# Column sums of a soft mixture in the logits' bank, dispatch weights turned ahead of the logits

## The chip, the core and the metric

One of the cores of a Trainium2 chip runs the whole program in fp32. The metric is device time in microseconds (us), the median of several runs. PE is TensorE, DVE is VectorE, ACT is ScalarE, POOL is GpSimd, SP is SyncE, which issues the transfers.

## The reference

Three layers follow each other. The middle of each is cut here to what is computed:

```python
attn = softmax(scale * q @ mean8(k).T);  x = attn @ mean8(v)   # 8 batches, 8 heads, 576 x 72, head size 64
r = np.maximum(x @ w_in, 0.0);  x = (r * r) @ w_out            # 4608 tokens, 512 -> 2048 -> 512
logits = x @ phi                                               # 4608 x 32 slots
d = np.exp(logits - logits.max(0));  d /= d.sum(0) + 1e-09     # over tokens
slot_input = d.T @ x                                           # 32 x 512, 4 slots for each of 8 experts
slot_out[e] = np.maximum(slot_input[e] @ w1[e], 0.0) @ w2[e]
c = np.exp(logits - logits.max(1));  c /= c.sum(1) + 1e-09     # over slots
return c @ slot_out
```

The maximum over tokens is only known at the end, so the kernel keeps a running maximum and running sums, which it rescales at each pair of tiles.

## The kernel before

**Tiles and units.** The 4608 tokens are 36 tiles (`NT`) of 128. The hidden layer of 2048 is cut into four quarters (`NQ`). A unit is one tile and one quarter: twelve 128x512 products on PE (`l1_half`, L453, weights and activations in high and low parts), then relu on ACT (L466) and the square on DVE (L473) or ACT (L475), which gives `g`. Units go two tiles at a time from tile 4 on; between them stand the other steps. The product with `w_out` is never made for a token: `phi` is folded into `w_out` (`a_sb`), and the sums over tokens are taken of `g`.

**The steps of a pair** (tiles t and t+1), each named by its function:

- `reload_turned` (L508) fetches the stored `g` back in a turned layout, `g_T` (L516) turns its 32x32 blocks on DVE.
- `logits` (L541) multiplies with `a_sb`, quarter by quarter. For tiles from 10 (`ND`) on, all quarters accumulate in the bank `pl`; then ACT copies the sum to `plsb` (L558). For tiles below 10, whose logits come late, each quarter takes a bank `att` and DVE adds it up (L556).
- `log_T` (L570) adds the four partial rows up and replicates the result with one product into the tile `lp`, in the bank `misc`. From `lp` come the maximum `m` (L573) and its running negative `nm` (L575) on DVE, the exponential `dT` with its sums `drs` (L582) and the rescaling factor `scl` (L588) on ACT, and on DVE four turns of the logits into `lt_sb` (L585) and the running sum `sn` (L590). `lt_sb` and `sn` are not needed until the end of the program; `dT` is needed at once.
- `d_T` (L605) turns `dT` in four pieces into `d`.
- `dg` (L615) multiplies `d` with the eight `g` of the pair into another tile of the bank `misc`; DVE then rescales and adds this to `acc` (L625). For the early pairs (0, 2, 4, 6 and 8) `g` has been fetched back from DRAM as `g_back`.

The names in the order of instructions below follow the tiles: `l_3717` is one tile of the bank `l1`, `pl`, `misc`, `att`, `gT` are banks, `turned` and `tmp` are buffers that hold the turned `g`.

**Banks.** PSUM has eight banks: two each for `l1`, `gT` and `att`, one for `misc`, one for `pl`.

**Attention beside it.** The tiles' attention runs in the same stream: `att_sc` (L234, L241, L245), the turning of the weights on DVE (L293), twelve block copies from there into the one buffer `aT` (`att_shift`: seven on ACT, L284, five on DVE, L286), the product with v (`att_av`, L311) and the split of its result into `xh` (L318, ACT) and `xl` (L319, DVE).

**What sets the order.** `at(slot, fn, ...)` puts a step into a numbered half unit, `run_slot` emits what is due there. The framework's scheduler then orders each engine's instructions by a simulated timeline. `tc.issue_after(x)` and, on top of it, `behind(names, fn)`, `pinned` and `behind_l1` hold a step back until another instruction, on the same engine, has been put in the order; `behind_l1` takes the last L453 product emitted so far. `post_end` sets the slots of `log_T`, `d_T` and `dg` of a pair, and puts `dg` of the pairs 10 to 26 behind such a product:

```python
        if ND <= t < NT - 8:
            at(s0 + p[2], behind_l1, dg, t)
```

**The end.** Tiles 34 and 35 are handled one by one: `log_T` of 34 uses `misc`, of 35 a bank of `l1`. After the last `acc`, PE turns it (L1010), ACT and DVE copy it to `accT` (L1014 `accT0`, L1015 `accT1`), PE multiplies with `w_out` (L1023), ACT scales the result with `rn` (L1031), and `rn` is the reciprocal of the last `sn` (L1018, L1019). From there the expert layers follow (L1046, L1078), the combination with c (L1107) and the stores of the output. Between these, `slot_weights_mm` (L650, PE) and `slot_weights_out` (L655 ACT, L656 DVE) prepare c, turned, as `cT`, and `slot_softmax` (L635 to L641) its last four tiles.

Of the kernel before, what the change touches and what calls it, by code (L numbers as in the profile page):

```python
# [8 lines left out]
F32 = mybir.dt.float32  # L9
# [3 lines left out]
ALU = mybir.AluOpType  # L13
# [4 lines left out]
def kernel(  # L18
# [12 lines left out]
    nc = tc.nc  # L31
# [3 lines left out]
    NSLOT = phi.shape[1]  # L35
# [4 lines left out]
    P = 128  # L40
    NT = NTOK // P
# [9 lines left out]
    ND = 10  # L51
# [13 lines left out]
    p2 = ctx.enter_context(tc.tile_pool(name="p2", bufs=2))  # L65
# [3 lines left out]
    ps1 = ctx.enter_context(tc.tile_pool(name="ps1", bufs=1, space=bass.MemoryType.PSUM))  # L69
# [14 lines left out]
    lt_sb = const.tile([P, NT, NSLOT], F32, tag="lt", name="lt_sb")  # L84
    acc = const.tile([P, QF], F32, tag="acc", name="acc")
# [6 lines left out]
    def ps(name):  # L92
        return ps2.tile([P, 512], F32, tag=name, name=name)

    def psm():
        return ps1.tile([P, 512], F32, tag="misc", name="misc")
# [265 lines left out]
    st_t, mark, n_st = {}, {}, [0]  # L362
# [44 lines left out]
    def natural(x):  # L407
        return x.rearrange("p (a c f) -> p c a f", a=4, f=32)
# [31 lines left out]
    hp_t, g_t, gT_t, L_t, dT_t, d_t, sc_d = {}, {}, {}, {}, {}, {}, {}  # L440
# [116 lines left out]
        elif alone or j == NQ - 1:  # L557
            nc.scalar.copy(out=dst, in_=pl)  # L558

    run, order = {}, []  # L560

    def width(t):
        return 1 if t >= NT - 2 else 2

    def log_T(t):
        w = width(t)
        order.append(t)
        pl = L_t.pop(t)[:, :w * P]
        lp = (ps("l1") if t == NT - 1 else psm())[:, :w * P]
        mark["log_T"] = nc.tensor.matmul(lp, s4rep.rearrange("p a b -> p (a b)"), pl)  # L570
        m = p2.tile([P, 1], F32, tag="m", name="m")
        nm = p2.tile([P, 1], F32, tag="nm", name="nm")
        nc.vector.reduce_max(out=m, in_=lp, axis=AX.X)  # L573
        if run:
            mark["nm"] = nc.vector.scalar_tensor_tensor(  # L575
                out=nm, in0=m, scalar=-1.0, in1=run["nm"], op0=ALU.mult, op1=ALU.min
            )
        else:
            nc.vector.tensor_scalar(out=nm, in0=m, scalar1=-1.0, scalar2=None, op0=ALU.mult)
        dT = p2.tile([P, 2, P], F32, tag="dT", name="dT")[:, :w]  # L580
        rs = p2.tile([P, 1], F32, tag="drs", name="drs")
        mark["exp"] = nc.scalar.activation(out=dT.rearrange("p u t -> p (u t)"), in_=lp, func=AF.Exp, bias=nm, accum_out=rs)  # L582
        for r in range(P // NSLOT):
            b = slice(r * NSLOT, (r + 1) * NSLOT)
            nc.vector.transpose(out=lt_sb[b, t:t + w], in_=lp[b].rearrange("p (u t) -> p u t", u=w)[:, :, b])  # L585
        if run:
            scl = p2.tile([P, 1], F32, tag="scl", name="scl")
            nc.scalar.activation(out=scl, in_=run["nm"], func=AF.Exp, bias=nm, scale=-1.0)  # L588
            sn = p2.tile([P, 1], F32, tag="sn", name="sn")
            nc.vector.scalar_tensor_tensor(  # L590
                out=sn, in0=run["s"], scalar=scl, in1=rs, op0=ALU.mult, op1=ALU.add
            )
            sc_d[t] = scl
            run["s"] = sn
        else:
            run["s"] = rs
        run["nm"] = nm
        dT_t[t] = dT

    def d_T(t):  # L600
        dT = dT_t.pop(t)
        d = p2.tile([P, 2, NSLOT], F32, tag="d", name="d")[:, :width(t)]
        for r in range(P // NSLOT):
            b = slice(r * NSLOT, (r + 1) * NSLOT)
            mark["d"] = nc.vector.transpose(out=d[b], in_=dT[b, :, b])  # L605
        d_t[t] = d

    def dg(t):
        d = d_t.pop(t)
        assert order.pop(0) == t  # L610
        dp = ps("gT") if t == NT - 1 else psm()
        for u in range(width(t)):
            for j in range(NQ):
                g = g_t.pop((t + u, j))
                mark["dg"] = nc.tensor.matmul(  # L615
                    dp[32 * j:32 * j + 32],
                    d[:, u],
                    g if t < NT - 4 else natural(g),
                    start=(u == 0),
                    stop=(u == width(t) - 1),  # L620
                )
        if t not in sc_d:
            nc.vector.tensor_copy(acc, dp)
        else:
            nc.vector.scalar_tensor_tensor(  # L625
                out=acc, in0=acc, scalar=sc_d.pop(t), in1=dp, op0=ALU.mult, op1=ALU.add
            )

# [33 lines left out]
    def behind(names, fn, *a):  # L662
        with ExitStack() as es:
            for n in names:
                es.enter_context(tc.issue_after(mark[n].ins))
            fn(*a)
# [82 lines left out]
    def at(slot, fn, *a):  # L749
        ev.setdefault(slot, []).append((fn, a))  # L750
# [5 lines left out]
    def run_slot(s):  # L756
        for fn, a in sorted(ev.pop(s, []), key=lambda e: e[0] is not logits):
            if fn in (g_T, logits, log_T, d_T, dg) and a[0] >= NT - EP:
                early(fn, *a)
            else:  # L760
                fn(*a)
# [19 lines left out]
    def post_end(t, s0, p):  # L781
        at(s0 + p[0], log_T, t)
        at(s0 + p[1], d_T, t)
        if ND <= t < NT - 8:
            at(s0 + p[2], behind_l1, dg, t)
        else:
            at(s0 + p[2], dg, t)
# [59 lines left out]
    for t in range(ND, NT - 2, 2):  # L847
        if t < NT - 4:
            post(t, SLOTS * t, (11, 13, 5))
        post_end(t, SLOTS * t, (26, 27, 28))  # L850
# [8 lines left out]
    for i in range(2):  # L859
        post_end(NT - 2 + i, s0, ((20, 21)[i],) * 3)  # L860
# [5 lines left out]
    for t in range(0, ND, 2):  # L866
        s0 = 96 + 28 * (t // 2)
        at(s0 - 4, reload_g, t)
        for n in range(2 * NQ):
            at(s0 - 3 + 3 * n, pinned, "store", reload_part, t, n // NQ, n % NQ)  # L870
        post(t, s0, (3, 6, -2), 4)
        post_end(t, s0, (20, 21, 23))
# [128 lines left out]
    behind(["log_T"], slot_weights_mm, 0, 2, 4)  # L1001
    behind(["log_T"], slot_weights_mm, 1, 0, 2)
    behind(["d"], slot_weights_mm, 1, 2, 4)
    behind(["exp", "nm"], slot_weights_out, 0)
    behind(["dg"], slot_weights_mm, 2, 0, 4)


# [5 lines left out]
    ptv = pt.rearrange("p (a b) -> p a b", b=P)  # L1013
    mark["accT0"] = nc.scalar.copy(out=accT[:, halves[0]], in_=ptv[:, halves[0]])  # L1014
    mark["accT1"] = nc.vector.tensor_copy(accT[:, halves[1]], ptv[:, halves[1]])  # L1015
    behind(["accT0", "accT1"], slot_weights_out, 1)
    behind(["accT0", "accT1"], slot_weights_out, 2)
    nc.vector.tensor_scalar(out=rn, in0=run["s"], scalar1=1e-9, scalar2=None, op0=ALU.add)  # L1018
# [138 lines left out]
```

## Time and profile before

| what | value |
|---|---|
| median of 3 runs | 779.25 us (777.89 to 781.28) |
| the profiled execution | 778.38 us, span 776.6 us |
| mean granted clock of PE | 0.972 of full speed |
| PE busy | 729.7 us, 94% of the span |
| weight loads on PE, DVE, ACT, POOL busy | 66%, 68%, 50%, 17% |
| the chain that ended last | PE 62%, DVE 14%, DMA 14%, ACT 4%, issue 3% |
| transfers | 174.17 MB on one hardware queue, 224 GB/s at the HBM over the span |

The busy share tells how full an engine is over the whole span, not what ends a wait. The table of waits names, for one engine, what it waited for and how long in total. The timeline gives single stretches: start, length, and in square brackets the idle time ahead with what ended it. Consecutive equal instructions stand there as one row with their count, and a row's length of a pipelined PE group is less than the sum of its members.

### The profile page before, as it was taken

What the parts mean: (1) busy time and instruction counts of PE and PEld (TensorE: products, weight loads), DVE (VectorE), ACT (ScalarE), POOL (GpSimd) and SP (SyncE); (2) the same over time, 40 slices, a digit from 0 to 9 for tenths busy, and PEclk for the clock granted to TensorE, in tenths of its full rate; (3) what the DMA queues carried; (4) which work ended last, traced back from release to release, by engine and by line L of the source; (5) the groups of instructions that cost most, each with busy time, mean ns of one, the idle gap of its engine ahead of it and who ended that gap; (6) DMA issues with size and microseconds to landing.
All of it is one profiled execution on the core that took longest, in us unless ns stands there. A gap on an engine that the chain in (4) does not pass through costs nothing.

```text
span 776.6 us, 14468 instructions
## 1 busy us (share of the span) xinstructions
PE 729.7 (94%) x5260; PEld 513.8 (66%) x5260; DVE 530.4 (68%) x1049; ACT 391.8 (50%) x1135; POOL 130.7 (17%) x151
## 2 busy tenths in 40 slices
PE   8789999989899999999999999989999999998993
PEld 7657788777677776577567666656666676663462
DVE  2996866596936688788868868877877655323243
ACT  2665577454547364535646552637475444331142
POOL 1232300051824400170231302410000000000000
PEclk7699999989999999999999999999999999999996
DMA  8955754757656997795898788768776326979988
GB/s 260 305 163 168 240 171 141 228 155 214 183 166 158 270 242 200 204 313 135 235 275 219 204 209 256 221 180 230 207 234 218 110 83 249 415 255 340 372 296 297
DMA packets 224135, 175.10 MB, mean 225 GB/s; under 512 B 75072, under 2 KB 186688, under 8 KB 224064
## 3 DMA queue, kind: packets, MB, share of 16 engines
q1 hardware_dynamic: 224064, 174.17, 74.4%
q8 instruction: 42, 0.69, 0.4%
q14 instruction: 29, 0.24, 0.1%
HBM read 126.94 MB, written 47.19 MB: 224 GB/s over the span
## 4 chain that ended last, share of the span: by engine, by line
PE 62%; DVE 14%; DMA 14%; ACT 4%; issue 3%; SPq 2%; POOL 1%; DVEq 0%; ACTq 0%; POOLq 0%
PE l L453 37%; DMA g_dram<-tmp 4%; PE misc L615 3%; DMA kv<-in_v_dram 2%; PE pl L541 2%; DMA tmp<-g_dram 2%; PE misc L1078 2%; PE l L1046 2%; PE att L164 2%; PE gT L311 2%; PE att L311 2%; PE att L234 2%; DMA out_dram<-o 1%; ACT es L245 1%; PE gT L234 1%
## 5 line engine op out<-in xcount | busy, mean ns | idle before, releaser
L453 PE MATMUL l<-w,xh 128*128 128x512 f32 x1152 | 385.2, 413 | 10.4 <-DVE g L473 5.0
L453 PEld LDWEIGHTS l<-w,xh 128*128 128x128 f32 x1152 | 209.1, 190 | 82.1 <-issue 17.6
L453 PE MATMUL l<-w,xl 128*128 128x512 f32 x576 | 230.7, 401 | 0.0
L466 ACT ACTIVATE r<-l 128x512 f32<-128x512 f32 x144 | 86.5, 603 | 176.4 <-PE l L453 165.1
L453 PEld LDWEIGHTS l<-w,xl 128*128 128x128 f32 x576 | 109.3, 190 | 28.8 <-issue 4.1
L157 POOL TENSOR_TENSOR kv<-kv 72x512 f32<-72x512 f32 x40 | 53.6, 1342 | 214.1 <-DMA kv<-in_k_dram 130.1
L284 ACT COPY aT<-turned 32x256 f32<-32x256 f32 (+1 forms) x168 | 67.8, 404 | 22.4 <-DVE turned L293 19.1
L473 DVE TENSOR_TENSOR g<-l,r 128x512 f32<-128x512 f32 x57 | 38.9, 683 | 29.0 <-ACT r L466 22.7
L516 DVE STREAM_TRANSPOSE turned<-turned 128x1024 f32<-128x1024 f32 x39 | 47.6, 1230 | 8.1 <-DMA turned<-g_dram 8.0
L245 ACT ACTIVATE es<-gT,mx 128x72 f32<-128x72 f32 x120 | 36.9, 333 | 19.0 <-DVE mx L241 19.0
L245 ACT ACTIVATE es<-att,mx 128x72 f32<-128x72 f32 x120 | 37.0, 335 | 12.9 <-DVE mx L241 12.7
L286 DVE COPY aT<-turned 32x256 f32<-32x256 f32 (+1 forms) x120 | 38.1, 318 | 1.5
L475 ACT ACTIVATE g<-r 128x512 f32<-128x512 f32 x54 | 34.4, 638 | 0.8
L473 DVE TENSOR_TENSOR tmp<-l,r 128x512 f32<-128x512 f32 x33 | 22.5, 682 | 17.9 <-ACT r L466 10.7
L396 POOL TENSOR_TENSOR w<-tmp,w 128x512 fp32r<-128x512 f32 x16 | 22.7, 1421 | 70.6 <-ACT w L395 62.4
L516 DVE STREAM_TRANSPOSE tmp<-tmp 128x1024 f32<-128x1024 f32 x25 | 30.3, 1224 | 5.8 <-DMA tmp<-g_dram 5.8
L158 POOL TENSOR_TENSOR kv<-kv 72x256 f32<-72x256 f32 x40 | 32.8, 825 | 0.8
L344 DVE TENSOR_SCALAR tmp<-tmp 128x512 uint32<-128x512 uint32 x32 | 16.0, 499 | 23.0 <-ACT tmp L342 22.9
L268 DVE TENSOR_TENSOR es<-es,rs 128x576 f32<-128x576 f32 x36 | 29.8, 830 | 0.7
L342 ACT ACTIVATE tmp<-st 128x512 f32<-128x512 f32 x32 | 21.5, 674 | 12.6 <-DMA st<-in_moe_w_in_dram 8.5
L615 PE MATMUL misc<-g,d 128*32 128x512 f32 x134 | 24.0, 596 | 3.9 <-DVE d L605 3.0
L245 ACT ACTIVATION_READ_ACCUMULATOR es<-att,mx 128x1 f32 x120 | 26.5, 221 | 0.0
(194 smaller groups left out, 1073.9 us busy)
## 6 DMA issues: line engine op xcount, KB each, us to landing
g_dram<-g SPq DMA_DIRECT2D x95, 256.0 KB
turned<-g_dram SPq DMA_DIRECT2D x39, 512.0 KB
w<-in_moe_w_dram SPq DMA_DIRECT2D x32, 512.0 KB
tmp<-g_dram SPq DMA_DIRECT2D x25, 512.0 KB
w<-in_moe_w_dram SPq DMA_DIRECT2D x6, 2048.0 KB
g_back<-g_dram SPq DMA_DIRECT2D x40, 256.0 KB
kv<-in_k_dram SPq DMA_DIRECT2D x32, 288.0 KB
kv<-in_v_dram SPq DMA_DIRECT2D x32, 288.0 KB
```

The lines of the kernel that those rows point to most:

```text
L157: eng.tensor_tensor(out=x[:, :, 0:4], in0=x[:, :, 0:4], in1=x[:, :, 4:8], op=ALU.add)
L158: eng.tensor_tensor(out=x[:, :, 0:2], in0=x[:, :, 0:2], in1=x[:, :, 2:4], op=ALU.add)
L245: mark["es", t] = nc.scalar.activation(out=es[:, e], in_=sv[:, h], func=AF.Exp, bias=mx[:, e:e + 1], accum_out=rsum[:, t % 8, e, 0:1],)
L284: nc.scalar.copy(out=dst, in_=src)
L286: eng[e].tensor_copy(dst, src)
L311: nc.tensor.matmul(px[e * D:(e + 1) * D, i * P + off:i * P + off + n], vp_t[b][:, 2 * i + e], aT[:, 2 * i + e, off:off + n],)
L453: mm = mark["l1", t, j] = nc.tensor.matmul(hp_t[t, j], steps[i][0], steps[i][1], start=(i == 0), stop=(i == 2 * n - 1))
L466: nc.scalar.activation(out=r, in_=hp, func=AF.Relu, scale=1.0 / (R * R if sq == "V" else R))
L473: mark["sq"] = nc.vector.tensor_tensor(out=dst, in0=pre, in1=src, op=ALU.mult)
L475: nc.scalar.activation(out=dst, in_=src, func=AF.Square)
L516: nc.vector.transpose(out=gc.rearrange("p (n i) -> p n i", i=32), in_=gc.rearrange("p (n f) -> p n f", f=32))
L615: mark["dg"] = nc.tensor.matmul(dp[32 * j:32 * j + 32], d[:, u], g if t < NT - 4 else natural(g), start=(u == 0), stop=(u == width(t) - 1),)
```

## The change

Three things change; no arithmetic does.

1. For the pairs 10 to 28, `log_T` takes its tile `lp` from the bank `pl` instead of `misc`. What follows `lp` without haste, the four turns into `lt_sb` and `sn`, is deferred (`rest`), and emitted behind the last of the four turns of `d_T`.
2. `dg` of the early pairs 0 to 8 is put behind an L453 product too.
3. For tiles 34 and 35, `lp` takes a bank of `l1`, and `rest` is emitted behind `accT1`. `slot_weights_out(0)` stands behind `acc` instead of behind `exp` and `nm`.

```diff
@@ log_T
-        lp = (ps("l1") if t == NT - 1 else psm())[:, :w * P]
+        if ND <= t < NT - 6:
+            lp = ps1.tile([P, 2 * P], F32, tag="pl", name="lp")
+        else:
+            lp = (ps("l1") if t >= NT - 2 else psm())[:, :w * P]
...
-        for r in range(P // NSLOT):
-            b = slice(r * NSLOT, (r + 1) * NSLOT)
-            nc.vector.transpose(out=lt_sb[b, t:t + w], in_=lp[b].rearrange("p (u t) -> p u t", u=w)[:, :, b])
+        old, scl = dict(run), None
         if run:
-            scl = p2.tile([P, 1], F32, tag="scl", name="scl")
+            scl = sc_d[t] = p2.tile([P, 1], F32, tag="scl", name="scl")
             nc.scalar.activation(out=scl, in_=run["nm"], func=AF.Exp, bias=nm, scale=-1.0)
-            sn = p2.tile([P, 1], F32, tag="sn", name="sn")
-            nc.vector.scalar_tensor_tensor(
-                out=sn, in0=run["s"], scalar=scl, in1=rs, op0=ALU.mult, op1=ALU.add
-            )
-            sc_d[t] = scl
-            run["s"] = sn
+            run["s"] = p2.tile([P, 1], F32, tag="sn", name="sn")
...
+        def rest():
+            for r in range(P // NSLOT):
+                b = slice(r * NSLOT, (r + 1) * NSLOT)
+                nc.vector.transpose(
+                    out=lt_sb[b, t:t + w], in_=lp[b].rearrange("p (u t) -> p u t", u=w)[:, :, b]
+                )
+            if old:
+                nc.vector.scalar_tensor_tensor(
+                    out=sn, in0=old["s"], scalar=scl, in1=rs, op0=ALU.mult, op1=ALU.add
+                )
+
+        if ND <= t < NT - 6:
+            rest_t[t] = rest
+        elif t >= NT - 2:
+            rests.append(rest)
+        else:
+            rest()
@@ d_T
+        if t in rest_t:
+            with tc.issue_after(mark["d"].ins):
+                rest_t.pop(t)()
@@ post_end
-        if ND <= t < NT - 8:
+        if t < NT - 8:
             at(s0 + p[2], behind_l1, dg, t)
@@ the end
-    behind(["exp", "nm"], slot_weights_out, 0)
+    behind(["acc"], slot_weights_out, 0)
...
+    for rest in rests:
+        behind(["accT1"], rest)
     behind(["accT0", "accT1"], slot_weights_out, 1)
```

The scheduler takes these as new data. Each engine's order is the same up to the first `log_T` (pair 10, at some 283 us), and differs in detail from there to the end. Line numbers shift: `lt_sb` L585 becomes L600, `sn` L590 becomes L604, `d` L605 becomes L620, `dg` L615 becomes L633, `acc` L625 becomes L643, `cT` L656 becomes L674.

The first place is PE at pair 14, from the replicating product (`log_T`) to the `dg` products. Before:

```order
L311 MATMUL gT<-aT,vp 64x128 x8
L570 MATMUL misc<-plsb,s4rep 128x256
L453 MATMUL l_3683<-w_745,xh 128x512 x2
...
L453 MATMUL l_3683<-w_745,xl 128x512
L453 MATMUL l_3717<-w_745,xh 128x512 x2
...
L541 MATMUL pl<-tmp,a_sb 32x256 x4
L453 MATMUL l_3717<-w_745,xh 128x512
...
L453 MATMUL l_3717<-w_745,xl 128x512
L311 MATMUL att<-aT,vp 64x128 x8
L541 MATMUL att<-tmp,a_sb 32x256 x4
L615 MATMUL misc<-g,d 32x512 x2
```

Now:

```order
L453 MATMUL l_3683<-w_745,xl 128x512
L311 MATMUL gT<-aT,vp 64x128 x8
L453 MATMUL l_3717<-w_745,xh 128x512
L573 MATMUL lp<-plsb,s4rep 128x256
L453 MATMUL l_3717<-w_745,xh 128x512
...
L453 MATMUL l_3717<-w_745,xl 128x512
L311 MATMUL att<-aT,vp 64x128 x8
L541 MATMUL att<-tmp,a_sb 32x256 x4
L633 MATMUL misc<-g,d 32x512 x2
...
L541 MATMUL pl<-tmp,a_sb 32x256 x4
L541 MATMUL att<-turned,a_sb 32x256 x4
L453 MATMUL l_3743<-w_243,xh 128x512 x2
```

Before, all twelve products of `l_3683` and all of `l_3717` stood between the two L311 groups; now the twelve of `l_3683` are done ahead of the first, and the first `logits` product of the next pair in `pl` has moved behind `dg`.

The second place is DVE at pair 20, from the turn of a reloaded `g` on. Before:

```order
L516 STREAM_TRANSPOSE tmp<-tmp 128x1024
L573 TENSOR_REDUCE m<-misc 128x1
L319 TENSOR_TENSOR xl<-att,xh 128x512
L575 SCALAR_TENSOR_TENSOR nm<-m,nm 128x1
L585 STREAM_TRANSPOSE lt_sb<-misc 32x64 x4
L605 STREAM_TRANSPOSE d<-dT 32x64
L590 SCALAR_TENSOR_TENSOR sn<-sn,scl,drs 128x1
L605 STREAM_TRANSPOSE d<-dT 32x64 x3
L556 TENSOR_TENSOR plsb<-plsb,att 128x2x4x32
```

Now:

```order
L516 STREAM_TRANSPOSE tmp<-tmp 128x1024
L319 TENSOR_TENSOR xl<-att,xh 128x512
L576 TENSOR_REDUCE m<-lp 128x1
L578 SCALAR_TENSOR_TENSOR nm<-m,nm 128x1
L620 STREAM_TRANSPOSE d<-dT 32x64 x4
L600 STREAM_TRANSPOSE lt_sb<-lp 32x64 x4
L604 SCALAR_TENSOR_TENSOR sn<-sn,scl,drs 128x1
```

The four turns of `d` now stand ahead of the four into `lt_sb`, and `xl` ahead of the maximum instead of behind it.

The third place is DVE at the end, from the maximum of tile 34 on. Before:

```order
L605 STREAM_TRANSPOSE d<-dT 32x32 x4
L585 STREAM_TRANSPOSE lt_sb<-misc 32x32 x4
L590 SCALAR_TENSOR_TENSOR sn<-sn,scl,drs 128x1
L573 TENSOR_REDUCE m<-l_7124 128x1
...
L625 SCALAR_TENSOR_TENSOR acc<-acc,scl,gT 128x512
L1015 COPY accT<-misc 128x256
```

Now:

```order
L576 TENSOR_REDUCE m<-l_7119 128x1
...
L643 SCALAR_TENSOR_TENSOR acc<-acc,scl,gT 128x512
L674 TENSOR_TENSOR cT<-att,cT 64x512
L1033 COPY accT<-misc 128x256
L600 STREAM_TRANSPOSE lt_sb<-l_7096 32x32 x4
L604 SCALAR_TENSOR_TENSOR sn<-sn,scl,drs 128x1
L600 STREAM_TRANSPOSE lt_sb<-l_7119 32x32 x4
L674 TENSOR_TENSOR cT<-att,cT 64x512
L604 SCALAR_TENSOR_TENSOR sn<-sn,scl,drs 128x1
L653 TENSOR_REDUCE cmx<-lt_sb 128x4
L674 TENSOR_TENSOR cT<-att,cT 64x512
L1038 TENSOR_SCALAR rn<-sn 128x1
```

Both tiles' turns into `lt_sb` and both `sn` have moved from ahead of the last `acc` to behind `accT1`, and `rn` with them.

## Rows read from the trace of the kernel before

**Rows 1.** Stretch, us, busy PE, PEld, DVE, ACT, POOL, clock, DMA; longest chain piece.

```profile
282.00:694.00 412.00, 401.43 (x2619) 271.02 (x2618) 300.24 (x629) 210.91 (x630) 53.09 (x66) 1.00 0.75 221
694.00:776.60 82.60, 64.19 (x839) 36.12 (x837) 31.17 (x70) 22.56 (x46) 0.00 (x0) 0.92 0.96 322
...
284.09 4.44 PE l L453 x19
```

**Rows 2.** Waits of PE over the whole span: us in total, times, longest us.

```profile
PE l L453 <- DVE g L473: 5.0, 3, 2.7
PE misc L615 <- DVE d L605: 4.4, 5, 1.3
```

**Rows 3.** Timeline of PE, starts of dg of pairs 2, 20, 6, 22, 26.

```profile
382.11 1.92 PE L615 MATMUL misc<-g_back,d 128*32 128x512 f32 x16 [1.33 <-DVE d L605]
471.31 0.62 PE L615 MATMUL misc<-g,d 128*32 128x512 f32 x2 [1.21 <-DVE d L605]
508.64 1.92 PE L615 MATMUL misc<-g_back,d 128*32 128x512 f32 x16 [1.46 <-DVE lt_sb L585]
511.47 0.62 PE L615 MATMUL misc<-g,d 128*32 128x512 f32 x2 [0.91 <-DVE acc L625]
588.55 0.62 PE L615 MATMUL misc<-g,d 128*32 128x512 f32 x2 [1.05 <-DVE d L605]
```

**Rows 4.** Timeline of DVE and ACT at pair 20.

```profile
465.96 1.25 DVE L516 STREAM_TRANSPOSE tmp<-tmp 128x1024 f32<-128x1024 f32 x1 [0.37 <-DMA tmp<-g_dram]
467.13 0.38 DVE L573 TENSOR_REDUCE m<-misc 128x1 f32<-128x256 f32 x1
468.44 0.47 ACT L582 ACTIVATE dT<-misc,nm 128x256 f32<-128x256 f32 x1 [4.27 <-DVE nm L575]
469.04 1.02 DVE L585 STREAM_TRANSPOSE lt_sb<-misc 32x64 f32<-32x64 f32 x4 [0.63 <-ACT dT L582]
470.43 0.74 DVE L605 STREAM_TRANSPOSE d<-dT 32x64 f32<-32x64 f32 x3
```

**Rows 5.** Timeline of PE and DVE at pair 14.

```profile
352.07 1.09 PE L311 MATMUL gT<-aT,vp 72*64 72x128 f32 x16
355.98 0.58 DVE L286 COPY aT<-turned 8x256 f32<-8x256 f32 x2
357.05 0.69 DVE L319 TENSOR_TENSOR xl<-gT,xh 128x512 fp32r<-128x512 f32 x1
361.56 0.60 PE L615 MATMUL misc<-g,d 128*32 128x512 f32 x2
363.28 0.61 PE L541 MATMUL att<-turned,a_sb 128*32 128x256 f32 x8
363.83 0.50 PE L453 MATMUL l<-w,xh 128*128 128x512 f32 x1
```

**Rows 6.** Timeline of all engines at the end.

```profile
696.00 0.49 PE L570 MATMUL l<-plsb,s4rep 128*128 128x128 f32 x2
696.50 0.89 DVE L585 STREAM_TRANSPOSE lt_sb<-misc 32x32 f32<-32x32 f32 x4
697.68 0.29 DVE L573 TENSOR_REDUCE m<-l 128x1 f32<-128x128 f32 x1
698.74 0.57 ACT L655 CAST cT<-att 128x512 fp32r<-128x512 f32 x1
702.51 0.75 DVE L625 SCALAR_TENSOR_TENSOR acc<-acc,scl,gT 128x512 f32<-128x512 f32 x1
704.88 3.64 PE L1023 MATMUL misc<-wot,accT 128*32 128x512 f32 x32 [0.92 <-DVE accT L1015]
705.05 0.69 DVE L656 TENSOR_TENSOR cT<-att,cT 64x512 fp32r<-64x512 f32 x1
708.59 0.69 ACT L1031 ACTIVATE si<-misc,rn 128x512 f32<-128x512 f32 x1 [2.18 <-PE misc L1023]
768.39 0.59 ACT L1111 COPY o<-att 128x512 f32<-128x512 f32 x1 [0.79 <-DMA out_dram<-o]
```

More of the change, by code (lines that the diff above doesn't have):

```diff
@@ L558, in logits @@
             nc.scalar.copy(out=dst, in_=pl)
-    run, order = {}, []
+    run, order, rest_t, rests = {}, [], {}, []
     def width(t):
@@ L598, in log_T @@
         dT_t[t] = dT
+        sn = run["s"]
+        def rest():
[14 more added lines that the diff above has]
+            rest()
     def d_T(t):
@@ L624, in dg @@
         else:
-            nc.vector.scalar_tensor_tensor(
+            mark["acc"] = nc.vector.scalar_tensor_tensor(
                 out=acc, in0=acc, scalar=sc_d.pop(t), in1=dp, op0=ALU.mult, op1=ALU.add
```

## Prediction

> **What bounds the kernel now.** I read the busy time by stretch first, since the orders are equal up to the first `log_T`. From 282 to 694 us, where the pairs are handled, PE is busy for 401.43 of 412 us at the full granted clock; DVE has 300.24 and ACT 210.91 [rows 1]. So PE bounds this stretch and only 10.57 us of it are idle: no shift of DVE or ACT work can bring more than that here, and work is neither added nor taken away (each engine has the same number of instructions before and now). From 694 us on it is otherwise: PE is busy for 64.19 of 82.6 us, and short steps on several engines wait for each other [rows 1]. Second, the table of waits says what the idle time is: `dg` waiting for `d` takes 4.4 us in five waits, an L453 product waiting for a square 5.0 us in three [rows 2]. Third, the timeline of PE places the waits of `dg`: pair 2 waits 1.33 us, pair 20 1.21, pair 26 1.05, all for `d`; pair 6 waits 1.46 us for the turns into `lt_sb`, which must leave the `misc` bank before `dg` may take it, and pair 22 0.91 us for the `acc` of the pair before, for the same bank [rows 3]. These five, 5.96 us, are what parts 1 and 2 of the change can reach. Last, the timelines around pair 20, pair 14 and the end [rows 4 to 6].
>
> The sum is made against the profiled execution, 778.38 us. That is 0.87 us under the median of 779.25, so its result is moved up by 0.87 to forecast a median. About 0.5% of the time, 3.9 us, is what a measurement can tell from no change: faster means below 775.35, slower above 783.15.
>
> **Part 1, pairs 10 to 28.** The turns of `d` no longer stand behind those into `lt_sb`. At pair 20 the `lt_sb` group takes 1.02 us and ends just before the last `d` [rows 4]. Now `xl` goes ahead of the maximum, but it stood between `m` and `nm` before, so `nm` and the exponential come when they came; `d` ends about 1.02 us sooner, and by the order there are three more products between `log_T` and `dg`. At 4.44 us for 19 products [rows 1] a product takes 0.234 us, so these are worth 0.7 us: with 1.02 they exceed the wait of 1.21 [rows 3]. **Pair 20: -1.2 us.** What the turns into `lt_sb` delay instead is the next pair's first product in `pl`, which now must wait for them. `d` takes about 0.98 us, `lt_sb` 1.02 behind it; the `dg` products run for 1.72 us (at pair 14 from 361.56 to 363.28 [rows 5]) to 1.92 us (pair 2 [rows 3]), and where the `pl` product comes behind `dg`, as it does in most pairs, that covers it. I cost this at nothing there; without the cover it would be up to 1.02 us a pair.
>
> Pair 26 has the same 1.02 us sooner `d`, but the L453 product behind `dg` waits for a square that DVE now does behind the turns into `lt_sb`: what `dg` gains is lost there. I take 0, between -1.05 (the whole wait goes [rows 3]) and 0.
>
> Pairs 6 and 22 stand close together. Their waits were 1.46 and 0.91 us [rows 3]. The first goes, since the logits of pair 22 no longer need `misc`, but now the `pl` product has to wait some 1.3 us (one `lt_sb` group and what is left of `d`), and `dg` of one still waits for the other's `acc`, about 0.5 of the 0.91. **-0.6 us**, between -2.37 and 0.
>
> At pair 14 the order is worse. Before, 24 products stood between the two L311 groups, now 12 fewer. The copies into the one `aT` buffer can only start once the first L311 group has read it, so what follows is a chain, counted from the end of that group (353.16 [rows 5]): the DVE copies end 3.40 us later, then `xl` 0.69 [rows 5], `m` 0.38 [rows 4] and `nm` some 0.2, the exponential until `lt_sb` could start 0.60 (468.44 to 469.04 [rows 4]), and `d` 1.0: 6.3 us. Then `dg` 1.72 and the two L541 groups, 0.61 and 0.55 [rows 5], of which one has moved here: 9.2 us, with handoffs 9.4. Before it was 10.67 us to the first product of the next unit (363.83 [rows 5]); without the 12 products, at 0.234 each, it would be 7.87. So PE has too little to do for about 1.5 us. **Pair 14: +1.5 us**, between 0 and 2.8 (the whole 12 products' worth).
>
> Pairs 10, 12, 16, 18, 24 and 28 showed no wait at `dg` and have as many products ahead of it as before: 0, each between 0 and 1.02 slower where the `lt_sb` group isn't covered. Pairs 30 and 32 are not touched.
>
> **Part 2, early pairs.** Only pair 2 had a wait for `d`, 1.33 us [rows 3]. Its `dg` now stands behind L453 products that don't need it, so the wait is covered: **-1.3 us**. The `g` it reads is held longer in `g_back`, and the next fetch into that buffer goes later on SP's queue; I see no wait of PE for it before and cost it at 0, at most the 1.33 back.
>
> **Part 3, the end.** The maximum of tile 35 started at 697.68, behind `lt_sb` and `sn` of tile 34, which take from 696.50 on [rows 6]. Now it starts as soon as its product is there: 696.00 + 0.49, so 1.1 us sooner. Of that 0.5 us is lost, since the ACT cast of `cT` (0.57) now goes ahead of the second exponential [rows 6]. With the `lt_sb` group of 35 and its `sn` gone from ahead of the last `acc` as well, the `acc` ends at some 700.85 where it ended at 703.26 (702.51 + 0.75), and the product with `w_out` starts at 702.5, not 704.88 [rows 6]: 2.4 us sooner. But `rn` now needs both deferred groups: from `accT1` at 702.45, two groups of 0.89, two `sn` of 0.22, two `cT` of 0.69, a reduction and a difference of some 0.29 each and two short steps of 0.15 [rows 6] come to some 4.5 us, with handoffs 4.7 (the short ones are estimates from the 0.29 of the maximum): `rn` at 707.15. The scaling with `rn` started at 708.59 [rows 6], its product would be ready at 706.2. So `rn` becomes the last, and **the end gains 1.4 us**, between 0 and 2.4. All behind it moves along; the last output copies wait 0.79 us for a buffer's store [rows 6], which follows PE's pace.
>
> **Sum:** -1.2 - 0.6 + 1.5 - 1.3 - 1.4 = -3.0 us. 778.38 - 3.0 = 775.4 for such an execution, **776.2 us** as a median.
>
> **Rivals.** (a) *Only the end gains.* The middle's gain is PE's, but DVE works in order and waits for reloaded `g`: the turn at 465.96 waits 0.37 us for its transfer [rows 4], and it stands ahead of pair 20's maximum. If PE runs sooner, that wait grows by as much, `d` comes no sooner and the gains of the middle cancel. Then 779.25 - 1.4 = 777.9 us. Against it: pairs 2 and 20 lie far apart and the waits for transfers are short.
>
> (b) *Slower: the shared bank.* One bank now holds a pair's logits, then its `lp`, then the next pair's logits, and the turns into `lt_sb` stand at the end of each turn. Where products run short as at pair 14, PE waits, 1.5 us each. If none of the middle's gains come and n pairs lose as pair 14 does, the time is 779.25 - 1.4 + 1.5n: it is slower by over 0.5% from four pairs on (783.9), and with five of the ten 785.4. The order shows one such pair; what speaks for more is that the order of every engine differs in detail from pair 10 on, and that in an engine's fixed order one late step holds up all behind it. What the rows show for `misc` is that this happens: pair 6's `dg` waited 1.46 us for a bank that was still being read [rows 3]. The Trainium skill (Perfetto Trace Analysis, Optimizing Tensor Performance, Matmuls) says that independent groups of products should rotate through different PSUM banks, so that one is emptied beside the next one's products. This change puts two groups that had two banks into one, against that rule, which by itself would speak for this rival; the wait of pair 6 agrees with it.
>
> (c) *More gain.* All five waits of `dg` go, 5.96 us, pair 14 finds cover, and the end gains 1.4: 779.25 - 7.4 = 771.9. If the rearranged order also shortens the 5.0 us of waits for squares [rows 2], it is more. For it: PE has no other large waits there. Against: the square is on DVE, which doesn't get less work.
>
> That the change doesn't do what it says can be left out: the order of instructions shows `d` ahead of `lt_sb` in each of the ten pairs.
>
> **How the numbers follow.** The sum (about 1.5 us to both sides): 0.43; of this some 0.16 lies below 775.35. (a) 0.17, all within 0.5%. (b) 0.15, slower. (c) 0.25, faster. So faster 0.41, same 0.44, slower 0.15. For the range I take in (c) with 1.4 us below it, 770.5, and most of (a)'s bounds and the smaller half of (b)'s, up to 782.5.
>
> **What would show it.** Right: no wait of `dg` for `d` over 0.3 us at pairs 2 and 20; a PE gap of about 1.5 us between the L311 groups and the next unit at pair 14; the first product with `w_out` 2.4 us sooner after tile 35's `log_T`, and its scaling waiting for `rn`. Wrong: PE idle above 10.57 us in the stretch of the pairs; waits of `pl` products for `lt_sb` in many pairs; or the scaling still waiting for its product.

## The result and the profile after

The changed kernel takes 770.15 us (median of 6 runs, 766.02 to 774.27); the kernel before took 779.61 beside it (777.42 to 781.28). The ratio is 0.9913, with a 95% interval of 0.9884 to 0.9943: 6.8 us faster, between 4.4 and 9.0. Measured once more later, the ratio was 0.9926 (0.9899 to 0.9953). The forecast was 776.2 us, a gain of 3.0, in a range from 770.5 to 782.5, with 0.44 for no change beyond 0.5% and 0.41 for faster. Applied to the 779.25 of the forecast, the ratio gives 772.5, which lies in the range; the raw median of these six runs lies 0.35 us below it. So the direction was right, the gain more than twice as large, and the likeliest class was the wrong one of two.

The two profiled executions lie further apart than that, 778.38 and 766.02 us. Part of it isn't the change. The first `log_T`, up to which both programs have the same order, starts at these times, first in the profile of before, then in that of after:

```profile
283.39 0.70 PE L570 MATMUL misc<-plsb,s4rep 128*128 128x256 f32 x2
```

```profile
278.32 0.70 PE L573 MATMUL lp<-plsb,s4rep 128*128 128x256 f32 x2
```

They are 5.07 us apart (the last section says more on this). I therefore read every run by two stretches of its profile: **M**, from this row to the `log_T` of tile 35, and **E**, from there to the end of the span. With 696.00 and a span of 776.6 [rows 6, time before], M was 412.61 and E 80.60; after, with 685.01 and a span of 764.24, they are 406.69 and 79.23. Busy time by stretch of the profile after (the rows of before are [rows 1]):

```profile
278.00:684.00 406.00, 399.60 (x2612) 272.12 (x2608) 302.13 (x631) 211.19 (x631) 53.89 (x66) 1.00 0.75 224
684.00:764.20 80.20, 62.74 (x834) 35.80 (x834) 30.57 (x68) 22.10 (x45) 0.00 (x0) 0.93 0.97 328
```

PE is idle for 6.40 us among the pairs, where it was idle for 10.57. The table of PE's waits over the whole span, which answers to [rows 2]:

```profile
PE l L453 <- DVE g L473: 5.0, 3, 2.7
PE l L453 <- DVE tmp L473: 1.6, 2, 1.2
PE misc L633 <- DVE d L620: 1.3, 3, 0.5
PE misc L633 <- DVE acc L643: 0.5, 1, 0.5
```

`dg` waited 4.4 us for `d` and now waits 1.3. The 5.0 us for squares are untouched; most of them were never in the stretch of the pairs: before, the three waits stand at 160.31 (1.93 us), 204.63 (2.68) and 450.05 (0.39), and only the last lies in M. Of the five waits of [rows 3], those of the pairs 2, 6 and 20 are gone, pair 22 keeps 0.48 of 0.91 and pair 26 0.52 of 1.05. What happened at the pairs 6 and 22 is the largest single piece. From pair 6's `log_T` to the first L453 product behind both pairs' `dg`, PE does the same 100 products in every run. Before, this lasts from 496.77 to 513.35, 16.58 us; after, from 489.51 to 503.99, 14.48 us (timeline of the profile after):

```profile
489.51 0.59 PE L573 MATMUL misc<-plsb,s4rep 128*128 128x256 f32 x2
491.05 0.70 PE L573 MATMUL lp<-plsb,s4rep 128*128 128x256 f32 x2
493.51 1.03 DVE L600 STREAM_TRANSPOSE lt_sb<-misc 32x64 f32<-32x64 f32 x4
496.30 0.41 DVE L576 TENSOR_REDUCE m<-lp 128x1 f32<-128x256 f32 x1
497.28 1.90 PE L633 MATMUL misc<-g_back,d 128*32 128x512 f32 x10
502.11 0.62 PE L633 MATMUL misc<-g,d 128*32 128x512 f32 x2 [0.48 <-DVE acc L643]
```

Pair 22's `log_T` starts 1.5 us behind pair 6's (491.05 and 489.51). Before, in the one bank `misc`, it had to stand behind the turns that read pair 6's `lp` (to 503.10), and came 8.3 us behind pair 6's (496.77 and 505.09); pair 6's `dg`, behind it in the same bank, then waited 1.46 us for pair 22's turns into `lt_sb` [rows 3]. That chain is gone: `dg` of pair 6 finds `misc` free, and DVE does pair 22's steps beside it.

The end, in the profile after (before: [rows 6]):

```profile
685.01 0.49 PE L573 MATMUL l<-plsb,s4rep 128*128 128x128 f32 x2
685.54 0.29 DVE L576 TENSOR_REDUCE m<-l 128x1 f32<-128x128 f32 x1
691.52 0.88 DVE L600 STREAM_TRANSPOSE lt_sb<-l 32x32 f32<-32x32 f32 x4
691.77 3.65 PE L1043 MATMUL misc<-wot,accT 128*32 128x512 f32 x32
695.49 0.15 DVE L1038 TENSOR_SCALAR rn<-sn 128x1 f32<-128x1 f32 x1
695.76 0.15 DVE L1039 RECIPROCAL rn<-rn 128x1 f32<-128x1 f32 x1
696.09 0.67 ACT L1051 ACTIVATE si<-misc,rn 128x512 f32<-128x512 f32 x1
```

Counted from `log_T` of tile 35, the product with `w_out` starts 6.76 us later instead of 8.88, and its scaling 11.08 instead of 12.59: 2.1 and 1.5 us sooner. `rn` is ready at 695.91 and is what the scaling waits for.

### The profile page after: what moved, and what is told of

It is laid out like the page before. It is cut to its first block, busy times and chain, and to the rows that moved or that the text cites. A ratio compares the mean times of both kernels' runs of the same rounds, so it can differ in the third digit from the quotient of the medians.

```text
span 764.2 us, 14453 instructions
## 1 busy us (share of the span) xinstructions
PE 723.5 (95%) x5260; PEld 511.4 (67%) x5260; DVE 532.0 (70%) x1049; ACT 392.1 (51%) x1135; POOL 132.1 (17%) x151
## 4 chain that ended last, share of the span: by engine, by line
PE 71%; DVE 12%; DMA 7%; ACT 6%; issue 2%; SPq 0%; POOL 0%; ACTq 0%; DVEq 0%
PE l L453 44%; PE misc L633 3%; PE pl L541 3%; PE misc L1098 2%; PE gT L311 2%; ACT es L245 2%; PE att L311 2%; PE l L1066 2%; PE gT L234 2%; PE att L234 2%; PE att L541 2%; DMA kv<-in_v_dram 1%; ACT aT L284 1%; DMA st<-in_moe_w_in_dram 1%; DMA out_dram<-o 1%
## 5 line engine op out<-in xcount | busy, mean ns | idle before, releaser
L453 PE MATMUL l<-w,xh 128*128 128x512 f32 x1152 | 383.4, 412 | 10.1 <-DVE g L473 5.0
L453 PEld LDWEIGHTS l<-w,xh 128*128 128x128 f32 x1152 | 209.8, 190 | 77.1 <-issue 17.1
L453 PE MATMUL l<-w,xl 128*128 128x512 f32 x576 | 231.7, 403 | 0.0
L453 PEld LDWEIGHTS l<-w,xl 128*128 128x128 f32 x576 | 109.3, 190 | 28.7 <-issue 3.9
L268 DVE TENSOR_TENSOR es<-es,rs 128x576 f32<-128x576 f32 x36 | 32.3, 902 | 0.7
L342 ACT ACTIVATE tmp<-st 128x512 f32<-128x512 f32 x32 | 21.7, 680 | 14.5 <-DMA st<-in_moe_w_in_dram 10.3
L245 ACT ACTIVATION_READ_ACCUMULATOR es<-gT,mx 128x1 f32 x120 | 26.0, 217 | 0.0
```

The costliest lines, as they stand in the source:

```text
L245: mark["es", t] = nc.scalar.activation(out=es[:, e], in_=sv[:, h], func=AF.Exp, bias=mx[:, e:e + 1], accum_out=rsum[:, t % 8, e, 0:1],)
L268: mark["norm", t] = nc.vector.tensor_tensor(out=es, in0=es, in1=rs.unsqueeze(2).to_broadcast([P, H, SP]), op=ALU.mult)
L453: mm = mark["l1", t, j] = nc.tensor.matmul(hp_t[t, j], steps[i][0], steps[i][1], start=(i == 0), stop=(i == 2 * n - 1))
```

## Experiments

All stretches below are read as above. The table has M and E of the kernels run, PE's busy time in M (by the same view as [rows 1]), its idle time (M less the busy time), and the ratio to the kernel before where a run was timed several times. The runs without a ratio have one execution each, and such single times don't compare kernels: early, which has the order of before, took 773.4 us, and before took 783.64 beside it.

| run | M | E | idle | PE busy | ratio |
|---|---|---|---|---|---|
| before | 412.61 | 80.60 | 11.1 | 401.5 | |
| early | 411.92 | 80.71 | 10.9 | 401.0 | |
| tail | 415.94 | 79.05 | 13.4 | 402.6 | |
| p1_defer | 412.13 | 80.89 | 9.7 | 402.4 | |
| p1_bank | 408.03 | 81.01 | 10.3 | 397.7 | |
| bank_gT | 408.21 | 80.96 | 6.7 | 401.5 | |
| p1_only | 408.56 | 80.70 | 8.2 | 400.4 | |
| the change | 406.69 | 79.23 | 6.5 | 400.1 | 0.9913 |
| after_again | 408.49 | 79.31 | 7.7 | 400.8 | 0.9926 (0.9899 to 0.9953) |
| after_sn | 409.28 | 78.67 | 7.7 | 401.6 | 0.9928 (0.9900 to 0.9957) |
| bank_sn | 407.79 | 78.75 | 8.5 | 399.3 | 0.9961 (0.9930 to 0.9993) |
| gT_sn | 410.77 | 78.80 | 7.1 | 403.7 | 0.9911 (0.9880 to 0.9943) |

M doesn't repeat exactly: up to the last two tiles, before, early and tail have one and the same order there, on every engine, and so have the change, p1_only, after_again and after_sn. The first group lies between 411.9 and 415.9 (mean 413.5), the second between 406.7 and 409.3 (mean 408.3).

Part of this scatter is PE's clock. In five profiles the granted clock falls to the lower of its two levels, 1.2 GHz, within M: for 3.4 us in tail, p1_defer, after_sn and bank_sn and for 6.8 us in gT_sn. In the other seven it is 2.4 GHz all through M. Two of the five, by the view of [rows 1], first p1_defer, then gT_sn:

```profile
502.92:506.33 3.41, 2.75 (x16) 0.68 (x16) 1.41 (x4) 0.00 (x0) 0.00 (x0) 0.50 0.44 110
421.93:428.76 6.83, 6.83 (x44) 5.61 (x45) 6.18 (x14) 2.71 (x7) 1.29 (x3) 0.50 0.64 177
```

Each time PE had just waited, or was waiting, for 1.6 to 2.6 us; but p1_bank has a wait of 1.8 us and keeps its clock, so the wait alone isn't shown to be the cause. PE's busy time in M is 1.2 to 1.5 us longer in the four runs, and 2.2 us in gT_sn, than in the runs of the same or the nearest order without a fall.

Without tail and after_sn the two groups have means of 412.3 and 407.9. So the middle gains 4.4 to 5.2 us, and with the end's 1.4 that is 5.8 to 6.6, beside the 6.8 of the timed runs. As two runs of one order lie up to 4.0 us apart, I take from a single run little more than which of the two groups it is in.

**Part 1 alone** (p1_only): the change with parts 2 and 3 undone,

```diff
-            lp = (ps("l1") if t >= NT - 2 else psm())[:, :w * P]
+            lp = (ps("l1") if t == NT - 1 else psm())[:, :w * P]
...
-        elif t >= NT - 2:
-            rests.append(rest)
...
-        if t < NT - 8:
+        if ND <= t < NT - 8:
             at(s0 + p[2], behind_l1, dg, t)
...
-    behind(["acc"], slot_weights_out, 0)
+    behind(["exp", "nm"], slot_weights_out, 0)
```

> Part 1 alone: pairs 10 to 28 take the logits' bank and defer their turns into lt_sb; the early dg and the end are as before. Read by two stretches of the profile, since the part ahead of the first log_T is the same program and still differed by 5.07 us between the two profiles: M, from log_T of pair 10 to log_T of tile 35 (before 412.61 us, after the whole change 406.69), and E, from there to the end of the span (before 80.6, after 79.2). Both theories: M is 1.2 above that of the whole change, since pair 2 keeps its wait: 407.9; E 80.6.

M is 408.56, E 80.70. M is 1.9 above the change's profile, but its order up to the last two tiles is the change's own, instruction for instruction, and pair 2 has no wait here either. So the difference is within what one order differs by between runs, and the expectation rested on a part that does nothing.

**Part 2 alone** (early): the kernel before with `if t < NT - 8:` in `post_end`.

> Part 2 alone: dg of the early pairs stands behind an L453 product. The wait of pair 2 (1.33 us) goes and nothing else changes: M 411.4, E 80.6. If the shifted fetches into g_back cost anything, M is 412 or more and pairs 4 to 8 show it.

It changes nothing at all: the order of every engine is the one before, and the wait stands (timeline of PE at pair 2, answering to the first of [rows 3]):

```profile
377.37 1.92 PE L615 MATMUL misc<-g_back,d 128*32 128x512 f32 x16 [1.07 <-DVE d L605]
```

The early `dg` already came behind those products. M is 0.69 lower with the same order. Pair 2's wait went with part 1, whose new order puts that `dg` elsewhere.

The three runs of before's order show something else: not every wait belongs to the order. Pair 2 waits 1.33, 1.07 and 0.78 us in before, early and tail, and pair 20 waits 1.21 us, not at all, and 0.41 us. The waits of the pairs 6, 22 and 26 are the same in all three within 0.03 us. Pair 20 in early, then in tail (their timelines of PE):

```profile
466.35 0.62 PE L615 MATMUL misc<-g,d 128*32 128x512 f32 x2
470.68 0.62 PE L628 MATMUL misc<-g,d 128*32 128x512 f32 x2 [0.41 <-DVE d L615]
```

**Deferral without the bank** (p1_defer): part 1 with `lp` left in `misc`.

```diff
-        if ND <= t < NT - 6:
-            lp = ps1.tile([P, 2 * P], F32, tag="pl", name="lp")
-        else:
-            lp = (ps("l1") if t == NT - 1 else psm())[:, :w * P]
+        lp = (ps("l1") if t == NT - 1 else psm())[:, :w * P]
```

> Only the deferral of part 1: d is turned ahead of lt_sb and sn in the pairs 10 to 28, lp stays in the bank misc. Theory W (the gain is that d comes 1 us sooner, so PE waits less at dg): M near that of part 1 alone, 408 to 409.5. Theory B (the gain is the bank: a pair's log_T no longer waits until dg has read the pair before it out of misc, and the first logits products of the next pair move next to others): M 411.4 to 412.6, with a wait at pairs 6 and 22 that stays over 1.5 us. E 80.6 by both.

M is 412.13, in the group of before: no gain is shown. The timeline of PE at the pairs 6 and 22:

```profile
503.58 3.26 PE L628 MATMUL misc<-g_back,d 128*32 128x512 f32 x16 [2.46 <-DVE lt_sb L597]
507.79 0.62 PE L628 MATMUL misc<-g,d 128*32 128x512 f32 x2 [0.94 <-DVE acc L638]
```

With `lp` still in `misc`, turning `d` first only means that `misc` is read out later: pair 6's wait for `lt_sb` grows from 1.46 to 2.46 us. During this wait the clock fell, and the 16 products of `dg` took 3.26 us instead of the 1.92 of [rows 3]. Over M, PE's idle time is 1.3 us below the mean of before and early and its busy time 1.2 us above it. Theory W, which wanted 409.5 at most, falls; a gain of about 1 us that the clock took back isn't excluded.

**The bank without the deferral** (p1_bank): part 1 with `rest()` always called at once in `log_T`.

```diff
-        if ND <= t < NT - 6:
-            rest_t[t] = rest
-        else:
-            rest()
+        rest()
```

> Only the bank of part 1: lp of the pairs 10 to 28 lies in the logits' bank, the turns into lt_sb and sn stay ahead of d. Theory W: d comes as late as before, so M 411 to 413, and the waits of dg for d at pairs 20 and 26 stay above 1 us each. Theory B: M 407.5 to 409, the wait at pairs 6 and 22 together under 0.7 us. E 80.6 by both.

M 408.03, as part 1. Theory B's M holds, its price at the pairs 6 and 22 doesn't: `dg` of 22 waits 1.8 us for `acc` there. PE's idle time is hardly below that of before; its busy time is 3.8 us lower. So this run reaches the length by another route than the change does. That made me ask whether the bank matters because it frees `misc` or because it holds back the next logits products until they stand together.

**Another bank** (bank_gT): as p1_bank, with

```diff
-            lp = ps1.tile([P, 2 * P], F32, tag="pl", name="lp")
+            lp = ps("gT")[:, :w * P]
```

> As the run with only the bank of part 1, but lp of the pairs 10 to 28 lies in a bank of gT: misc is freed as there, and the logits' bank too, so the next pair's first logits products need not wait for lp. Theory F (the gain is that misc is free): M (first log_T to last) falls by 3 us or more from before's 411.9 to 412.6. Theory J (the gain is that the logits products are held back until they stand next to other short groups, so that PE changes less often between kinds of products): M stays within 1 us of before, and PE's time without its idle gaps in the units 54 to 142 stays at 390.3 to 390.8 us (bank alone: 387.0).

M 408.21, PE busy as before (401.5; from the start of unit 54 to that of unit 142, without the idle gaps, 390.8) and idle 4.4 us less. Theory F holds: that `lp` leaves `misc` is enough, with the logits' bank left alone. Joined groups don't cause it here; that they do in p1_bank, whose busy time is 3.8 us lower, is likely, but not shown. The waits of `dg` for `d` that the deferral was to remove are partly there in this run, 1.05 us at pair 20 and 1.35 at pair 24 (the expectation of gT_sn below calls the second one pair 8, wrongly), and M is short all the same:

```profile
469.72 0.62 PE L628 MATMUL misc<-g,d 128*32 128x512 f32 x2 [1.05 <-DVE d L615]
```

What joined groups are worth can be read apart, at pair 24, where neither the run early nor the change has a wait of PE. The stretch from `log_T` to the next L204 group holds the same 74 products in both. In early:

```profile
532.13 0.59 PE L570 MATMUL misc<-plsb,s4rep 128*128 128x256 f32 x2
535.46 0.64 PE L541 MATMUL pl<-turned,a_sb 128*32 128x256 f32 x8
535.91 0.60 PE L541 MATMUL att<-turned,a_sb 128*32 128x256 f32 x4
536.44 0.73 PE L453 MATMUL l<-w,xh 128*128 128x512 f32 x2
...
541.02 0.59 PE L541 MATMUL att<-turned,a_sb 128*32 128x256 f32 x2
543.05 0.41 PE L204 MATMUL att<-ident,kp 72*128 72x72 f32 x4
```

and in the change:

```profile
527.03 0.59 PE L573 MATMUL lp<-plsb,s4rep 128*128 128x256 f32 x2
535.45 0.61 PE L541 MATMUL pl<-turned,a_sb 128*32 128x256 f32 x8
535.88 0.61 PE L541 MATMUL att<-turned,a_sb 128*32 128x256 f32 x8
...
537.00 0.42 PE L204 MATMUL att<-ident,kp 72*128 72x72 f32 x4
```

10.92 us against 9.97: with the second logits group in one piece, next to the first and to `dg`, PE needs 0.95 us less for the same work. It repeats: tail has 10.92 and p1_defer 10.91, p1_bank and p1_only have 9.97. The profile of before, with early's order, has 11.39 (536.80 to 548.19), also without a wait that its timeline shows, so not all that a stretch can lose is seen as a wait. That the changes between kinds of products cost this is my reading; no run changes only them. Over M, PE's busy time averages 401.7 us in the first group of runs and 400.7 in the second (401.2 and 400.4 without tail and after_sn), so about 1 us of the gain may be of this kind and some 3.5 to 4.3 us are idle time that went.

**Part 3 alone** (tail): the kernel before with the third part of the diff only.

> Part 3 alone. If the parts add up, E is 79.2 us as with the whole change (before 80.6 to 80.9) and M is before's 411.9 to 412.6. If the end only gained through what the middle left behind, E stays above 80.5.

E 79.05: the end's gain adds to the middle's. M came out at 415.94, outside the expectation, with before's order. Against the mean of before and early it is 3.7 us longer: 2.4 us more idle time and 1.3 us more busy time. There are two waits ahead of pair 6, of 1.25 and 2.18 us, that the profile of before doesn't have, behind a turn at which DVE waits 5.26 us for its reload (2.71 before), and 1.8 us behind the second one the clock falls.

**sn at once at the end** (after_sn): the change, with `sn` of the last two tiles behind their `d`.

```diff
         def rest():
...
-            if old:
+            if t < NT - 2:
+                add_s()
...
             rests.append(rest)
+            sums.append(add_s)
...
+        if sums:
+            with tc.issue_after(mark["d"].ins):
+                sums.pop(0)()
```

(`add_s` holds the addition that made `sn`.)

> The whole change, but sn of tiles 34 and 35 is not deferred: each stands right behind its d, and only the turns into lt_sb wait for accT1. If rn ends last at the end, as the sum had it, the scaling of the product with w_out now waits for that product alone and E is 0.5 to 0.7 us under that of the change: 78.6. If not, E stays at 79.2. M 406.7 to 408.6 as before this edit (two runs of the same middle).

E 78.67, 0.56 below the change's 79.23. The scaling now starts 0.25 us behind the end of its product, where the change let it wait 0.67:

```profile
700.28 3.64 PE L1051 MATMUL misc<-wot,accT 128*32 128x512 f32 x32
704.17 0.67 ACT L1059 ACTIVATE si<-misc,rn 128x512 f32<-128x512 f32 x1
```

So `rn` was last, as the sum had it. The total doesn't show 0.6 us: 0.9928 against 0.9913 and 0.9926. M, 409.28, lies above the expected 408.6; a late reload (last section) and a fall of the clock make this run longer.

**The two edits combined with the other banks** (bank_sn: after_sn without the deferral in the pairs; gT_sn: after_sn with `lp` of the pairs in a bank of `gT`).

> As the run before, with sn not deferred at the end, and no deferral in the pairs 10 to 28: only their bank changes. If the order of d and lt_sb is worth nothing there, the time is that of the whole change with sn within 1.5 us: M 407.5 to 408.5, E 78.6. If d ahead of lt_sb is worth its 1.02 us at the pairs where dg waits for d, it is 2 us slower.

> The whole change with sn not deferred at the end, but lp of the pairs 10 to 28 in a bank of gT instead of the logits' bank. The run with only that bank reached M 408.21 and kept waits of dg for d of 1.05 us at pair 20 and 1.35 at pair 8. If the deferral has a worth of its own once misc is free, pair 20's wait falls under 0.3 us and M is 406 to 407.5, E 78.7, and the time is 1 to 2 us under that of the whole change. If the freed misc bank is all that counts, M stays at 408.2 within the 1 us that two runs of one order differ, and the time is the whole change's.

bank_sn: M 407.79, E 78.75, as expected if the deferral is worth nothing, and the medians differ by 0.9 us (771.36 and 770.48), but its ratio is 0.33% above after_sn's, 2.6 us, with intervals that overlap; this stays undecided. gT_sn: the wait of `dg` at pair 20 is gone, yet M is 410.77, which neither branch of the expectation has. PE waits 2.57 us at 421.85 for copies into `aT` that DVE makes late, behind a reloaded `g` (its timeline), and right behind this wait the clock falls for 6.8 us. In all, M has 0.4 us more idle time than that of bank_gT and 2.2 us more busy time, so most of the excess goes with the clock:

```profile
416.88 1.25 DVE L516 STREAM_TRANSPOSE turned<-turned 128x1024 f32<-128x1024 f32 x1 [2.77 <-DMA turned<-g_dram]
```

Its ratio of 0.9911 can't be told from the change's. None of the three was shown to beat the change.

**The change once more** (after_again).

> The whole change once more, on the same chip as the run before. It measures how far one order repeats: M so far was 406.69, 408.56 and 409.28 in three profiles with the same order of the middle, and E was 79.23. Expected: M between 406.7 and 409.3, E 79.1 to 79.3, about 0.9% under the kernel before.

M is 408.49, as expected, E 79.31, at the upper end. The gain is 0.74%, where 0.9% was expected.

## Why the prediction was right or wrong

- **The sum's direction, and rival (c).** The time came nearest to (c), 771.9 us, but by another route: of the five waits only three went wholly, pair 14 did not find cover, and the joined groups added about 1 us. That the range holds the time is luck in part: its lower end came from (c), and two of the sum's three parts were wrong.
- **Part 1 was mis-sized: -0.3 us (-1.2 - 0.6 + 1.5), measured -4.4 to -5.2, with pair 2's wait in it.** The step that failed is the one that took the earlier `d` for what the part brings. Alone, the earlier `d` shows no gain (p1_defer), and with `lp` out of `misc` M is as short with `d` as late as before (p1_bank, bank_gT; one profile each). I had seen `misc` as the reason for the waits at the pairs 6 and 22, and priced it at 0.6, with 1.3 us of new wait for the `pl` product set against it. The two `log_T` could now follow each other at once, and the stretch from the first of them to the first L453 product behind both `dg` went from 16.58 us (before, early) to 14.48 in three of the four runs of the new order and 14.59 in the fourth. The 2.1 us there, 0.95 at pair 24, up to 1.3 each at the pairs 2 and 20, less the loss at pair 14, are most of what M gained; each edit moves much of the order, and which move brings the rest stays open.
- **Pair 20: -1.2 forecast, between -1.2 and 0 measured.** The wait is gone, but it was not a fixed one: early and tail, with before's order, have 0 and 0.41 us. The sum took a wait of one profile for a property of the order.
- **Pair 14: +1.5 forecast, 0.7 measured, and 0.9 to 1.2 in the other runs of this order.** In the profile after, PE waits 0.27 us at the second L311 group and 0.39 at the first product of the next unit, and that unit starts 8.48 us behind the end of the first L311 group (350.41 to 358.89), where I had 9.4, and 7.87 would have been without loss. The term taken wrongly is the 3.40 us until the DVE copies end: I carried it over from [rows 5], but with other turns ahead of them those copies end 1.8 us after the group now (350.76 + 1.47 in the timeline after).
- **Part 2: -1.3 forecast, nothing measured.** The wait went, but the edit alone doesn't move an instruction; the change as a whole had to be taken apart to see that. I took the cover from the change's order and credited the line of the diff that seemed to say it.
- **Pair 24 and joined groups: 0 forecast.** The sum knew only waits, and took PE's idle 10.57 us for all that there was to gain. The 0.95 us at pair 24 have no wait beside them, and p1_bank's busy time in M is 3.8 us below that of before, with the same products in another order.
- **Squares.** The prediction read the 5.0 us of [rows 2] as idle time of the pairs' stretch, and (c) counted on them for more; only 0.39 us of them lie there.
- **Part 3: -1.4 forecast, -1.4 measured in E and -1.5 at the scaling.** The step by step working held: product sooner by 2.1 (2.4 forecast), `rn` last, scaling sooner by 1.5.
- **Pair 26: 0 forecast, 0 measured.** Its wait halved, and the next L453 product waits 1.16 us where it waited 0.63, as the step said.
- **Rival (a)** is seen, but not as a limit: a reload that comes late lengthens single runs of an order (below), and the middle gains all the same.
- **Rival (b)** fell. The logits' bank is shared now, and of the pairs only 14 loses. Where `lp` goes, to `pl` or to the two banks of `gT`, made no difference in M (408.03 and 408.21), though the two runs get there differently. The Trainium skill (Perfetto Trace Analysis, Optimizing Tensor Performance, Matmuls) has the rule to rotate independent groups of products through different PSUM banks. I had held it against the change; the runs agree with it once it is applied to the bank that is left: `misc` had held two pairs' `lp` and both their `dg`.

## What to carry to other kernels

Ask first whose buffer an operation leaves, and who can start because of it; how soon its own result comes may matter less. Before a wait goes into a sum, see in a second profile of the same order whether it is there again. When a change has several parts and a scheduler orders the work, compare the orders part by part: a line of the diff can be without any effect, and another can take the credit it doesn't have. And a wait-by-wait sum for a full engine should say that it leaves out what the order does to the busy time; here that was about 1 us.

## What the runs showed that was not expected

- The same order took 411.9 to 415.9 us in M. Besides the clock, one difference of this kind, in two runs of the change's order, is whether a reload has landed when DVE comes to it. In the run after_sn, where PE then waits 2.13 us at 427.10 for a square and the clock falls at 428.59, and, at the same place, in the profile after:

```profile
419.26 1.25 DVE L516 STREAM_TRANSPOSE turned<-turned 128x1024 f32<-128x1024 f32 x1 [2.69 <-DMA turned<-g_dram]
```

```profile
411.75 2.36 DVE L516 STREAM_TRANSPOSE turned<-turned 128x1024 f32<-128x1024 f32 x2
```

- Of the 5.07 us between the two profiles ahead of the change, 4.15 are there at the first L453 product already (35.82 and 31.67). Up to it the granted clock was 0.72 of full speed in before and 0.87 after. PEclk of the page in 40 slices, first before, then after, has 0.7 and 0.9 in its first slice:

```profile
PEclk7699999989999999999999999999999999999996
```

```profile
PEclk9699999999999999999999999999999999999997
```

Whether the clock is the cause of all of it was not tried.
